# A long convolution, a LayerNorm and a two-row expert on one core: loads on one queue, a new order, two row writes

## The chip, the cores and the metric

The kernel runs on one core of one Trainium2 chip. The metric is the device time of one execution in microseconds. A core has five engines with their own instruction streams: PE (matmul, with PEld as its weight loads), DVE, ACT, POOL and SP, which here only issues DMAs. All inputs and the output are bfloat16 in HBM.

## The reference

S = 2048 tokens, D = 640 channels, F = 1728, four taps in the shift filter, two selected tokens.

```python
def _A_ref(q, k, v, shift_k, ssm_k, ssm_D):
    # k_shift: causal 4-tap filter along the tokens, one filter per channel
    kv = k_shift * v
    # y: causal convolution of kv with ssm_k along 2048 tokens, by FFT of length 2 S
    y = y + kv * ssm_D[None, None, :]
    return q * y

def _B_ref(x, w_r, w_gate, w_up, w_down):
    r = x @ w_r
    idx = jnp.argsort(-r, axis=-1)[:, :2]          # the two tokens of highest score
    g = _silu(x_sel @ w_gate); u = x_sel @ w_up
    y = (g * u) @ w_down * _sigmoid(r_sel)
    return x + scatter(y)                          # two rows change

h = A_q + _A_ref(_layernorm(A_q), A_k, A_v, A_shift_k, A_ssm_k, A_ssm_D)
h2 = h + _B_ref(_layernorm(h), B_w_r, B_w_gate, B_w_up, B_w_down)
```

`B_x` is not used.

## The kernel before

The 640 channels are worked in five chunks c of 128, and the tokens as 16 columns n2 of 128. The convolution is a transform of length 4096 in two steps each way, all as matmuls. For a chunk the groups of PE are: FT (transposes of the filter, 16 matmuls), S1f (first transform step of the filter, four groups of 16), KT (transposes of k), SC (the shift filter as matmuls with diagonal matrices, two groups), S1k (first step of k times v, four groups of 16), S2p (second step of both, eight groups of 16), I1 and I2 (the two inverse steps), T (transposes of h). Each group writes one of four PSUM regions; ACT or DVE then copies or multiplies the region into SBUF (`copyflex`, L334, recorded at L335). For chunk 0 the four taps use four diagonals. For chunks 1 to 4 two shifted copies of k are stacked in one tile (`Pst`); six SBUF to SBUF DMAs per chunk build them (`b_KT`), and SC needs all six. The filter spectrum is swapped between partition halves (`st_swap`, into KfB), by SP's DMA or DVE's copy for each half; DVE multiplies spectra (P1, P2). DVE and ACT make the first LayerNorm's sums of x (`ln0`), POOL normalises (L779). The last chunk's I2 goes in three parts of 8, 4 and 4 token columns (`LPARTS`), before and after.

The second LayerNorm's sums come from Gram matmuls (`b_G`, G0 to G4, small matmuls on transposed h, L822 and L827); G0 and G1 stand together after chunk 3's I1 groups. Then follow scores, the top two, the gather of the two rows by one-hot matmuls, the FFN (L1000, L1025), and `rows`, the two new rows. Meanwhile `outn` normalises all tokens, four bulk writes (`Dout`) store them, and `Dfix` writes the two rows over, when the bulk writes have landed.

Every step is declared once with the engines it may use (`decl`, `op`, `flex`, `dma`). The table `PLAN` then gives, step by step, the order, the engine and the PSUM region: an entry is 64 times the step's number plus 8 times the engine's number plus the region. `plan` derives the semaphore waits, `replay` emits each engine's stream. The order in an engine's stream is thus fixed: an instruction that waits holds all that stand behind it, SP's DMA issues too. In the diff `sp/act` lists the engines that a DMA may be issued from; the entry of `PLAN` says which it is.

Of the kernel before, what the change touches and what calls it, by code (L numbers as in the profile page):

```python
# [300 lines left out]
def build(nc, A_q, A_k, A_v, A_shift_k, A_ssm_k, A_ssm_D, B_x, B_w_r, B_w_gate, B_w_up, B_w_down, out):  # L301
# [8 lines left out]
    with es:  # L310
# [145 lines left out]
        def ld_filt(c):  # L456
            dma("sp/act", filt_C, A_ssm_k[CW * c:CW * c + CW, :], 1.35, writes=[buf("fC")], name="fC%d" % c)

        def ld_tok(c, nm, tile, src):
            w = min(2, NCH - c) * CW  # L460
            for i in range(2):
                a, b = 8 * i, 8 * i + 8
                dma("sp/act" if c == 0 else "sp", tile[:, a:b, 0:w], src[:, a:b, CW * c:CW * c + w], 1.75 if w > CW else 1.3,
                    writes=[buf(nm, j, i) for j in range(w // CW)], name="%s%d%d" % (nm, c, i), nd=1024)
# [7 lines left out]
        dma("sp/act", cons[:], I_d.ap(), 0.4, writes=[bI], name="cons")  # L472
# [4 lines left out]
        dma("sp/act/pool", tiny[:, 0:512], A_shift_k.rearrange("(c p) j -> c (p j)", c=NCH), 0.1, writes=[buf("ty", 0)] + bBp, name="wC", nd=5)  # L477
        dma("sp/act/pool", tiny[:, 512:640], A_ssm_D.rearrange("(c p) -> c p", c=NCH), 0.1, writes=[buf("ty", 1)], name="DC", nd=5)
        dma("sp/act/pool", tiny[:, 640:768], B_w_r.rearrange("(c p) -> c p", c=NCH), 0.1, writes=[buf("ty", 2)], name="wr", nd=5)
# [11 lines left out]
        dma("sp/act", F1[:].rearrange("p c k -> p (c k)"), F1_d.ap(), 0.4, writes=[bF1], name="F1")  # L491
        for h in range(2):
            dma("sp/act", F2c[:, 64 * h:64 * h + 64].rearrange("p k c m -> p (k c m)"), F2_d.ap()[:, 2048 * h:2048 * h + 2048], 1.4,
                writes=allq[0:4] if h == 0 else allq[3:7], name="F2c%d" % h)
# [645 lines left out]
```

## Time and profile before

| what | value |
|---|---|
| timed runs | 152.9, 154.67, 155.04 us (median 154.67) |
| profiled execution | 153.12 us, its span 151.3 us |
| busy PE, DVE, ACT, POOL | 118.6, 119.5, 111.2, 24.3 us |
| mean granted PE clock | 0.928 of full speed |
| moved by DMA | 29.54 MB, mean 195 GB/s |

The span is the time from the first to the last instruction of the program; the execution's own time has 1.8 us around it. Times in the profile count from the start of the span. Busy shares are averages over stages with different limits; the chain of waits says what ended last at each step.

### The profile page before, as it was taken

Reading aid. Unit: us, or ns where it says so; the run is one execution under the profiler, and the core shown is the slowest. Engines: PE = TensorE matmul, PEld = TensorE weight load, DVE = VectorE, ACT = ScalarE, POOL = GpSimd, SP = SyncE. Lnnn points to the kernel's source line nnn. Section 1 sums busy time; section 2 is a strip of 40 time slices with the busy share of each in tenths; the row PEclk is TensorE's granted clock in tenths of the full one; section 3 lists DMA queues with packets and bytes.
Section 4 is the critical chain, followed back from the end, with each engine's and each line's share of the span. In section 5 each row is a group of like instructions: output and inputs, shape, how many; then the busy total and the mean of one; then the engine's idle time right before and its main releaser. Section 6 shows DMA issues by size and latency. Waiting matters only on the chain.

```text
span 151.3 us, 6739 instructions
## 1 busy us (share of the span) xinstructions
PE 118.6 (78%) x3063; PEld 109.5 (72%) x3063; DVE 119.5 (79%) x186; ACT 111.2 (73%) x129; POOL 24.3 (16%) x29
## 2 busy tenths in 40 slices
PE   2504976895958879899999999998999199844991
PEld 2504975895947768799989899977999188733981
DVE  0379859997769997789888999889989465969812
ACT  0336999998559978899897998787999157229910
POOL 2003101005889994000000000000000000000000
PEclk9985799999999999999999999999999999995555
DMA  4999996999998838892659923378089950000970
GB/s 98 398 402 313 273 290 207 258 223 348 185 223 178 258 80 178 189 232 77 139 110 191 226 48 69 74 236 349 11 270 388 359 208 4 0 6 4 390 308 5
DMA packets 20900, 29.54 MB, mean 195 GB/s; under 512 B 5761, under 2 KB 16200, under 8 KB 20424
## 3 DMA queue, kind: packets, MB, share of 16 engines
q1 hardware_dynamic: 19566, 27.98, 64.1%
q10 hardware_dynamic: 1274, 1.13, 2.3%
q8 instruction: 24, 0.39, 1.1%
q14 instruction: 4, 0.03, 0.1%
q0 software_dynamic: 32, 0.00, 0.0%
HBM read 19.60 MB, written 2.62 MB: 147 GB/s over the span
## 4 chain that ended last, share of the span: by engine, by line
PE 56%; ACT 12%; DMA 11%; issue 9%; DVE 7%; SPq 3%; DVEq 0%; ACTq 0%
PE ps L600 10%; PE ps L644 7%; DMA x_sb<-in_A_q_dram 6%; PE ps L689 6%; PE ps L707 6%; PE ps L690 5%; PE ps L575 5%; ACT big L335 4%; DMA big<-big 4%; SPq L331 3%; PE ps L550 3%; PE ps L1000 3%; PE ps L581 2%; PE ps L728 2%; ACT A L335 2%
## 5 line engine op out<-in xcount | busy, mean ns | idle before, releaser
L335 ACT ACTIVATE big<-ps 128x1024 bf16<-128x1024 f32 (+2 forms) x40 | 42.6, 1112 | 7.5 <-PE ps L600 6.3
L335 ACT ACTIVATE A<-ps 128x1024 bf16<-128x1024 f32 x28 | 26.7, 1028 | 1.9 <-PE ps L644 1.9
L600 PE MATMUL ps<-F,big 128*64 128x128 bf16 x640 | 22.7, 221 | 4.3 <-issue 2.5
L644 PE MATMUL ps<-big,F 128*128 128x64 bf16 x640 | 21.5, 193 | 2.7 <-ACT big L335 1.3
L600 PEld LDWEIGHTS ps<-F,big 128*64 128x64 bf16 x640 | 18.7, 110 | 6.6 <-issue 2.9
L644 PEld LDWEIGHTS ps<-big,F 128*128 128x128 bf16 x640 | 19.8, 98 | 4.1 <-ACT big L335 2.0
L335 ACT ACTIVATE Bp<-ps 128x1024 bf16<-128x1024 f32 x17 | 16.9, 1035 | 7.9 <-PE ps L690 7.9
L779 POOL TENSOR_SCALAR q_sb<-x_sb,ln 128x640 bf16<-128x640 bf16 x16 | 19.5, 1218 | 11.5 <-DVE ln L776 10.0
L689 PE MATMUL ps<-G,A 128*128 128x128 bf16 x160 | 19.1, 219 | 0.2 <-ACT Bp L335 0.2
L690 PE MATMUL ps<-G,KfB 128*128 128x128 bf16 x160 | 19.0, 219 | 0.0
L717 DVE TENSOR_TENSOR atmp<-q_sb,ps 128x1024 bf16<-128x1024 bf16 (+1 forms) x11 | 12.3, 1122 | 5.5 <-PE ps L707 5.4
L689 PEld LDWEIGHTS ps<-G,A 128*128 128x128 bf16 x160 | 15.5, 98 | 0.9 <-ACT Bp L335 0.4
L690 PEld LDWEIGHTS ps<-G,KfB 128*128 128x128 bf16 x160 | 15.7, 98 | 0.0
L585 DVE TENSOR_TENSOR big<-ps,big 128x1024 bf16<-128x1024 f32 x10 | 12.2, 1224 | 4.2 <-PE ps L575 2.6
L335 DVE CAST A<-ps 128x1024 bf16<-128x1024 f32 x12 | 14.2, 1217 | 0.1
L665 DVE TENSOR_TENSOR A<-A 128x2048 bf16<-128x2048 bf16 x10 | 12.8, 1285 | 1.4 <-DMA KfB<-A 1.4
L707 PE MATMUL ps<-Bp,H 128*128 128x128 bf16 x160 | 10.7, 220 | 3.5 <-issue 3.0
L754 DVE BATCH_NORM_STATS2 st<-x_sb 128x6 f32<-128x320 bf16 x22 | 9.0, 479 | 4.0 <-DMA x_sb<-in_A_q_dram 4.0
L707 PEld LDWEIGHTS ps<-Bp,H 128*128 128x128 bf16 x160 | 9.0, 98 | 4.3 <-issue 3.2
L673 DVE TENSOR_TENSOR KfB<-A,KfB 128x2048 bf16<-128x2048 bf16 x10 | 12.1, 1217 | 0.0
L575 PE MATMUL ps<-diag,big 128*128 128x64 bf16 x256 | 8.6, 193 | 1.8 <-DMA big<-big 1.5
L335 ACT ACTIVATE q_sb<-ps 128x2048 bf16<-128x2048 bf16 (+2 forms) x5 | 7.4, 1472 | 3.1 <-PE ps L728 3.1
(119 smaller groups left out, 169.1 us busy)
## 6 DMA issues: line engine op xcount, KB each, us to landing
x_sb<-in_A_q_dram SPq DMA_DIRECT2D x4, 640.0 KB, 7.6
KfB<-A SPq DMA_DIRECT2D x5, 512.0 KB, 4.3
out_dram<-q_sb SPq DMA_DIRECT2D x4, 640.0 KB, 3.9
big<-big SPq DMA_DIRECT2D x8, 260.0 KB, 6.4
big<-in_A_v_dram SPq DMA_DIRECT2D x4, 512.0 KB, 8.1
big<-in_A_ssm_k_dram SPq DMA_DIRECT2D x4, 512.0 KB, 6.4
big<-big SPq DMA_DIRECT2D x8, 243.8 KB, 6.4
big<-in_A_k_dram SPq DMA_DIRECT2D x3, 512.0 KB, 8.7
```

The source lines that it names most:

```text
L335: return flex(lambda e: e.activation(o, i(), ACTF.Copy), lambda e: e.tensor_copy(o, i()), reads, writes, (t_act(n), t_d2(n) if bf else t_d ...
L575: return e.matmul(R32(bt)[:, o:o + 64], lhsT=lt, rhs=diagS[:, s, h, a, :], start=(a == 0), stop=(a == 1))
L585: op("dve", lambda e: e.tensor_tensor(kv[:, :, 8 * hb:8 * hb + 8, :], R32(bt).rearrange("p (n g l) -> p g n l", n=8, l=4), v_T[:, 8 * hb:8 ...
L600: return e.matmul(R32(bt)[64 * cc:64 * cc + 64, 128 * gl:128 * gl + 128], lhsT=lt, rhs=F1[:, cc, :], start=True, stop=True, tile_position= ...
L644: bt = op("pe", [lambda e, kl=kl: e.matmul(R32(bt)[:, 64 * kl:64 * kl + 64].rearrange("p (s g) -> p s g", s=2), lhsT=F2[:, 16 * r + kl, :] ...
L665: op("dve", lambda e: e.tensor_tensor(dst[:, :, blk], A[:, :, blk], dst[:, :, blk], ALU.mult), reads=[buf("A2", ksl(c), r) for r in rs], w ...
L673: return lambda e: e.tensor_tensor(K[:, g0:g1, blk], A[:, g0:g1, blk], K[:, g0:g1, blk], ALU.mult)
L689: ems.append(lambda e, g=g, gl=gl: e.matmul(R32(bt)[:, 128 * gl:128 * gl + 128], lhsT=dst[:, g, :], rhs=G[:, 0, :], start=True, stop=False))
L690: ems.append(lambda e, g=g, gl=gl: e.matmul(R32(bt)[:, 128 * gl:128 * gl + 128], lhsT=K[:, g, :], rhs=G[:, 1, :], start=False, stop=True))
L707: ems.append(lambda e, n2=n2, nl=nl, cp=cp: e.matmul(R32(bt)[:, 128 * nl:128 * nl + 128], lhsT=H[:, n2, cp, :], rhs=Bp[:, 16 * cp + n2, :] ...
L717: tr.decl({"dve": lambda e: e.tensor_tensor(at, qv, R32(bt)[:, 0:128 * nn].rearrange("p (n d) -> p n d", n=nn), ALU.mult)}, qb, ab, {"dve" ...
L779: lambda e, n2=n2: e.tensor_scalar(q_sb[:, n2, :], x_sb[:, n2, :], rd[:, n2:n2 + 1], nb[:, n2:n2 + 1], op0=ALU.mult, op1=ALU.add),
```

## The change

Four things are changed.

- The bulk loads (filter, first k and v, constants, the masks' source F2c, the weights) may now be issued by SP alone; the three tiny loads (`wC`, `DC`, `wr`) by ACT or POOL alone.
- `PLAN` is another table. It moves steps on all engines.
- The transposes of the two new rows (`YT`) are in two groups, of three and two, and their copy (`rows`) is in two: 384 columns on DVE, 256 on ACT.
- The row number of the second row is loaded on ACT, and ACT issues its write; SP keeps the first row.

```diff
 PLAN = [
-    32, 1248, 1744, 1424, 2960, 2832, 1120, 2512, 2896, 456, 1184, 1312, 536, 2384, 2704, 2576, 2448, 1472, 416, 577, 656, 720, 328, 5392, 5442, 2768,
...
+    1120, 1424, 392, 520, 2512, 2384, 2448, 2320, 1560, 1472, 1248, 3016, 472, 32, 577, 656, 10456, 1744, 720, 2896, 352, 5384, 1312, 3080, 3144, 800,
...
-            dma("sp/act", filt_C, A_ssm_k[CW * c:CW * c + CW, :], 1.35, writes=[buf("fC")], name="fC%d" % c)
+            dma("sp", filt_C, A_ssm_k[CW * c:CW * c + CW, :], 1.35, writes=[buf("fC")], name="fC%d" % c)
...
-                dma("sp/act" if c == 0 else "sp", tile[:, a:b, 0:w], src[:, a:b, CW * c:CW * c + w], 1.75 if w > CW else 1.3,
+                dma("sp", tile[:, a:b, 0:w], src[:, a:b, CW * c:CW * c + w], 1.75 if w > CW else 1.3,
...
-        dma("sp/act/pool", tiny[:, 0:512], A_shift_k.rearrange("(c p) j -> c (p j)", c=NCH), 0.1, writes=[buf("ty", 0)] + bBp, name="wC", nd=5)
+        dma("act/pool", tiny[:, 0:512], A_shift_k.rearrange("(c p) j -> c (p j)", c=NCH), 0.1, writes=[buf("ty", 0)] + bBp, name="wC", nd=5)
...
-        pt = op("pe", [lambda e, t=t: e.transpose(R16(pt)[0:2, 128 * t:128 * t + 128], yv[:, t, :], ident) for t in range(NCH)],
-                reads=[buf("yv", 0), buf("yv", 1), bI], region=True, dur=0.45, name="YT")
-        op("dve", lambda e: e.tensor_copy(rows, R16(pt)[0:2, 0:D]), writes=[buf("rows")] + bBp, uses=pt, dur=0.48, name="rows")
+        pt = op("pe", [lambda e, t=t: e.transpose(R16(pt)[0:2, 128 * t:128 * t + 128], yv[:, t, :], ident) for t in range(3)],
+                reads=[buf("yv", 0), buf("yv", 1), bI], region=True, dur=0.3, name="YT")
+        op("pe", [lambda e, t=t: e.transpose(R16(pt)[0:2, 640 + 128 * t:768 + 128 * t], yv[:, t, :], ident) for t in range(3, NCH)],
+           reads=[buf("yv", 0), buf("yv", 1), bI], writes=[buf("yt1")], uses=pt, dur=0.2, name="YT")
+        tr.decl({"dve": lambda e: e.tensor_copy(rows[:, 0:384], R16(pt)[0:2, 0:384])}, [], [buf("rows", 0)], {"dve": 0.32}, uses=pt, name="rows", after=bBp)
+        tr.decl({"act": lambda e: e.activation(rows[:, 384:D], R16(pt)[0:2, 1024:1280], ACTF.Copy)}, [buf("yt1")], [buf("rows", 1)], {"act": 0.38}, uses=pt, name="rows", after=bBp)
...
-            for cc in range(2):
-                t = tr.decl({"sp": lambda e, cc=cc: e.dma_start(out[0][bass.ds(vals[cc], 1), :], rows[cc:cc + 1, :])},
-                            [buf("rows")], [buf("fix", cc)], {"sp": 0.45}, dma=0.1, name="Dfix", after=[buf("outp", i) for i in range(4)])
+            for cc, g in enumerate(("sp", "act")):
+                def ldidx(e, cc=cc):
+                    vals[cc] = e.value_load(idxcol[cc:cc + 1, 0:1], min_val=0, max_val=S - 1)
+                t_ld = tr.decl({g: ldidx}, [buf("idxcol")], [], {g: 0.9}, name="LDI", silent=True)
+                t = tr.decl({g: lambda e, cc=cc: e.dma_start(out[0][bass.ds(vals[cc], 1), :], rows[cc:cc + 1, :])},
+                            [buf("rows", 0), buf("rows", 1)], [buf("fix", cc)], {g: 0.45}, dma=0.1, name="Dfix", after=[buf("outp", i) for i in range(4)])
```

The two helpers whose engine lists change alike (`F1`, `F2c`, `cons`, the weights `wg`, `wu`, `wd`) are left out.

What the table moves is seen in the engines' streams. SP at the start of the program; `in_A_q` is x, `in_A_ssm_k` the filter, `c_F2` the masks' source, `big<-big` a stack copy. Before:

```order
L331 DMA cons<-c_I 128x324
L331 DMA x_sb<-in_A_q_dram 128x2560 x4
L331 DMA Bp<-in_A_shift_k_dram 5x512
L331 DMA big<-in_A_k_dram 128x8x256
L331 DMA F1<-c_F1 128x256
L331 DMA q_sb<-c_F2 128x2048
L331 DMA big<-in_A_v_dram 128x8x256
L331 DMA q_sb<-c_F2 128x2048
L331 DMA big<-in_A_v_dram 128x8x256
L331 DMA big<-in_A_ssm_k_dram 128x2048
L331 DMA big<-in_A_k_dram 128x8x256 x2
L331 DMA big<-big 64x1950
```

After:

```order
L331 DMA x_sb<-in_A_q_dram 128x2560 x2
L331 DMA cons<-c_I 128x324
L331 DMA big<-in_A_ssm_k_dram 128x2048
L331 DMA x_sb<-in_A_q_dram 128x2560
L331 DMA F1<-c_F1 128x256
L331 DMA x_sb<-in_A_q_dram 128x2560
L331 DMA big<-in_A_k_dram 128x8x256
L331 DMA q_sb<-c_F2 128x2048
L331 DMA big<-in_A_k_dram 128x8x256
L331 DMA q_sb<-c_F2 128x2048
L331 DMA big<-in_A_v_dram 128x8x256 x2
```

The first filter chunk and half of the first k, which ACT issued before, are now in SP's row; behind the last row shown stand the second filter chunk, one k load (before: two) and the six stack copies.

PE at the start, behind its first transposes: L523 is FT, L545 and L550 KT, L600 S1, L581 SC of chunk 0. Before:

```order
L523 MATMUL ps<-cons,big 128x128 x16
L545 MATMUL ps<-cons,big 128x128 x16
L600 MATMUL ps<-F1,big 64x128 x48
L581 MATMUL ps<-diag,big 128x128 x32
L600 MATMUL ps<-F1,big 64x128 x16
L550 MATMUL ps<-cons,big 128x128 x16
L581 MATMUL ps<-diag,big 128x128 x32
L600 MATMUL ps<-F1,big 64x128 x64
```

After:

```order
L523 MATMUL ps<-cons,big 128x128 x16
L600 MATMUL ps<-F1,big 64x128 x48
L545 MATMUL ps<-cons,big 128x128 x8
L600 MATMUL ps<-F1,big 64x128 x16
L545 MATMUL ps<-cons,big 128x128 x8
L550 MATMUL ps<-cons,big 128x128 x16
L581 MATMUL ps<-diag,big 128x128 x64
L523 MATMUL ps<-cons,big 128x128 x16
```

The filter's S1 groups went ahead of the transposes of k, and chunk 0's two SC groups stand together.

SP near the end, the weights and the last swap. Before:

```order
L622 DMA KfB<-A2 64x4096
L331 DMA big<-in_B_w_gate_dram 128x3x1728
L331 DMA big<-in_B_w_up_dram 128x2x1728
L331 DMA big<-in_B_w_down_dram 128x4x640 x2
L331 DMA misc<-c_misc 128x320
L331 DMA big<-in_B_w_up_dram 128x3x1728
L331 DMA big<-in_B_w_down_dram 128x5x640
L331 DMA big<-in_B_w_gate_dram 128x2x1728
```

After:

```order
L622 DMA KfB<-A2 64x4096 x2
L331 DMA big<-in_B_w_gate_dram 128x2x1728
L331 DMA big<-in_B_w_down_dram 64x640
L331 DMA big<-in_B_w_down_dram 128x4x640
L331 DMA big<-in_B_w_up_dram 128x2x1728
L331 DMA big<-in_B_w_down_dram 128x4x640
L331 DMA big<-in_B_w_gate_dram 128x3x1728
L331 DMA big<-in_B_w_up_dram 128x3x1728
L331 DMA big<-in_B_w_down_dram 128x5x640
```

The first row of `w_down` waits for the last readers of the tile A1, the S2p groups of chunk 4, and holds the rows behind it; before, the two loads of `w_gate` and `w_up` stood ahead of that wait. Both halves of chunk 3's swap are DMAs now.

## Rows read from the trace of the kernel before

**Rows 1.** The page: busy us (share) xinstructions; a DMA queue's packets, MB, engines' share.

```profile
PE 118.6 (78%) x3063; PEld 109.5 (72%) x3063; DVE 119.5 (79%) x186; ACT 111.2 (73%) x129; POOL 24.3 (16%) x29
...
q8 instruction: 24, 0.39, 1.1%
```

**Rows 2.** Stages: length, busy us (xinstructions) PE, PEld, DVE, ACT, POOL; clock, DMA, GB/s.

```profile
25.00:37.00 12.00, 8.40 (x244) 7.78 (x244) 11.58 (x14) 11.94 (x12) 1.85 (x2) 1.00 1.04 285
...
45.00:62.00 17.00, 13.74 (x361) 12.46 (x360) 15.89 (x13) 15.01 (x16) 12.63 (x11) 1.00 0.74 176
...
62.00:98.00 36.00, 35.67 (x873) 33.47 (x871) 32.21 (x32) 32.05 (x34) 0.00 (x0) 1.00 0.61 135
```

**Rows 3.** Chain of waits, 0 to 37 us: start, length, what ended.

```profile
2.64 9.79 DMA x_sb<-in_A_q_dram
...
25.06 1.88 ACT big L335
...
30.45 6.29 DMA big<-big
```

**Rows 4.** Timeline of SP, 20 to 32 us: start, length, what it issued.

```profile
23.31 1.01 SPq L331 DMA_DIRECT2D big<-in_A_k_dram  x2
...
26.96 4.09 SPq L331 DMA_DIRECT2D big<-big  x6
```

**Rows 5.** Chain of waits, the whole span.

```profile
42.04 1.67 issue
...
49.26 0.36 issue
...
114.53 0.30 PE ps L822 x32
...
116.81 1.17 PE ps L707 x19
...
117.97 3.03 issue
```

**Rows 6.** DMA queues, 115.1 to 121 us: packets, MB, share of 16 engines.

```profile
q1 hardware_dynamic: 1023, 2.08, 98.3%
...
q8 instruction: 1, 0.02, 1.2%
```

**Rows 7.** DMA packets, 0 to 12 us.

```profile
DMA packets 1657, 3.62 MB, mean 301 GB/s; under 512 B 143, under 2 KB 1017, under 8 KB 1657
```

**Rows 8.** Groups by line and form: busy us, mean ns of one.

```profile
L335 ACT ACTIVATE big<-ps 128x2048 bf16<-128x2048 bf16 x4 | 7.5, 1884 | 1.0 <-PE ps L550 0.8 <-PE ps L581 0.2
...
L335 ACT ACTIVATE A<-ps 128x1024 bf16<-128x1024 f32 x28 | 26.7, 1028 | 1.9 <-PE ps L644 1.9
...
L335 DVE COPY big<-ps 128x2048 bf16<-128x2048 bf16 x5 | 6.1, 1223 | 1.8 <-PE ps L523 1.2 <-PE ps L550 0.6
...
L335 DVE CAST A<-ps 128x1024 bf16<-128x1024 f32 x12 | 14.2, 1217 | 0.1
...
L754 DVE BATCH_NORM_STATS2 st<-x_sb 128x6 f32<-128x320 bf16 x22 | 9.0, 479 | 4.0 <-DMA x_sb<-in_A_q_dram 4.0
```

**Rows 9.** The page's DMA issues: KB each, median us to landing.

```profile
KfB<-A SPq DMA_DIRECT2D x5, 512.0 KB, 4.3
```

**Rows 10.** Timeline of PE, 5 to 37 us.

```profile
14.08 1.93 PE L523 MATMUL ps<-cons,big 128*128 128x128 bf16 x16 [0.88 <-DVE big L521]
...
23.07 1.95 PE L581 MATMUL ps<-diag,big 128*128 128x128 bf16 x32
...
28.32 1.21 PE L523 MATMUL ps<-cons,big 128*128 128x128 bf16 x16
```

**Rows 11.** Timeline, from 139 us: the output writes and the row copy.

```profile
139.24 5.41 SPq L331 DMA_DIRECT2D out_dram<-q_sb  x4
...
148.68 0.48 DVE L1037 COPY Bp<-ps 2x640 bf16<-2x640 bf16 x1 [0.79 <-PE ps L1035]
...
149.34 0.72 SPq L1058 DMA_DIRECT2D out_dram<-Bp  x2
```

More of the change, by code (lines that the diff above doesn't have):

```diff
@@ L470, in ld_v @@
             ld_tok(c, "vT", v_T, v3)
-        dma("sp/act", cons[:], I_d.ap(), 0.4, writes=[bI], name="cons")
+        dma("sp", cons[:], I_d.ap(), 0.4, writes=[bI], name="cons")
         ld_k(0)
@@ L476, in build @@
         bBp = [buf("Bp", gb) for gb in range(4)]
-        dma("sp/act/pool", tiny[:, 0:512], A_shift_k.rearrange("(c p) j -> c (p j)", c=NCH), 0.1, writes=[buf("ty", 0)] + bBp, name="wC", nd=5)
-        dma("sp/act/pool", tiny[:, 512:640], A_ssm_D.rearrange("(c p) -> c p", c=NCH), 0.1, writes=[buf("ty", 1)], name="DC", nd=5)
-        dma("sp/act/pool", tiny[:, 640:768], B_w_r.rearrange("(c p) -> c p", c=NCH), 0.1, writes=[buf("ty", 2)], name="wr", nd=5)
+        dma("act/pool", tiny[:, 0:512], A_shift_k.rearrange("(c p) j -> c (p j)", c=NCH), 0.1, writes=[buf("ty", 0)] + bBp, name="wC", nd=5)
+        dma("act/pool", tiny[:, 512:640], A_ssm_D.rearrange("(c p) -> c p", c=NCH), 0.1, writes=[buf("ty", 1)], name="DC", nd=5)
+        dma("act/pool", tiny[:, 640:768], B_w_r.rearrange("(c p) -> c p", c=NCH), 0.1, writes=[buf("ty", 2)], name="wr", nd=5)
         ty4 = tiny[:, 0:512].rearrange("q (p j) -> q p j", j=4)
@@ L490, in build @@
         op("dve", lambda e: e.tensor_copy(D32[:], wDr[:, 8, :]), reads=[buf("DC")], writes=[buf("D32")], dur=0.17, name="D32")
-        dma("sp/act", F1[:].rearrange("p c k -> p (c k)"), F1_d.ap(), 0.4, writes=[bF1], name="F1")
+        dma("sp", F1[:].rearrange("p c k -> p (c k)"), F1_d.ap(), 0.4, writes=[bF1], name="F1")
         for h in range(2):
-            dma("sp/act", F2c[:, 64 * h:64 * h + 64].rearrange("p k c m -> p (k c m)"), F2_d.ap()[:, 2048 * h:2048 * h + 2048], 1.4,
+            dma("sp", F2c[:, 64 * h:64 * h + 64].rearrange("p k c m -> p (k c m)"), F2_d.ap()[:, 2048 * h:2048 * h + 2048], 1.4,
                 writes=allq[0:4] if h == 0 else allq[3:7], name="F2c%d" % h)
@@ L888, in build @@
                 WB[nm].append(bw)
-                dma("sp/act", wsb[:, a:b, :], src.rearrange("(t p) f -> p t f", p=128)[:, a:b, :], 1.1 * (b - a), after=wbufs(base + a * Ff, base + b * Ff), writes=[bw], name=nm, nd=128 * (b - a))
+                dma("sp", wsb[:, a:b, :], src.rearrange("(t p) f -> p t f", p=128)[:, a:b, :], 1.1 * (b - a), after=wbufs(base + a * Ff, base + b * Ff), writes=[bw], name=nm, nd=128 * (b - a))
         base = 2 * NCH * Ff
@@ L894, in build @@
             WB["wd"].append(bw)
-            dma("sp/act", wd_sb[:, a:b, :], B_w_down[128 * a:128 * b, :].rearrange("(t p) d -> p t d", p=128), 0.45 * (b - a), nd=128 * (b - a),
+            dma("sp", wd_sb[:, a:b, :], B_w_down[128 * a:128 * b, :].rearrange("(t p) d -> p t d", p=128), 0.45 * (b - a), nd=128 * (b - a),
                 after=wbufs(base + a * D, base + b * D), writes=[bw], name="wd")
@@ L898, in build @@
         WB["wd"].append(bw)
-        dma("sp/act", wd_sb[0:FL, NFT - 1, :], B_w_down[128 * (NFT - 1):Ff, :], 0.5, after=wbufs(base + (NFT - 1) * D, W_SZ), writes=[bw], name="wd")
+        dma("sp", wd_sb[0:FL, NFT - 1, :], B_w_down[128 * (NFT - 1):Ff, :], 0.5, after=wbufs(base + (NFT - 1) * D, W_SZ), writes=[bw], name="wd")
         for c in range(NCH - 1):
@@ L1049, in build @@
         if FIXSP:
-            vals = []
-            def ldidx(e):
-                for cc in range(2):
-                    vals.append(e.value_load(idxcol[cc:cc + 1, 0:1], min_val=0, max_val=S - 1))
-            t_ld = tr.decl({"sp": ldidx}, [buf("idxcol")], [], {"sp": 2.0}, name="LDI", silent=True)
-            t_fix = []
-            for cc in range(2):
-                t = tr.decl({"sp": lambda e, cc=cc: e.dma_start(out[0][bass.ds(vals[cc], 1), :], rows[cc:cc + 1, :])},
-                            [buf("rows")], [buf("fix", cc)], {"sp": 0.45}, dma=0.1, name="Dfix", after=[buf("outp", i) for i in range(4)])
+            vals = {}
+            t_fix = []
+            for cc, g in enumerate(("sp", "act")):
[4 more added lines that the diff above has]
+                            [buf("rows", 0), buf("rows", 1)], [buf("fix", cc)], {g: 0.45}, dma=0.1, name="Dfix", after=[buf("outp", i) for i in range(4)])
                 t.preds.add(t_ld.tid)
@@ L1063, in build @@
             t_fix = [tr.decl({"pool": lambda e: e.indirect_dma_start(out[0], bass.IndirectOffsetOnAxis(idxcol, 0), rows, None)},
-                             [buf("rows"), buf("idxcol")], [buf("outp", i) for i in range(4)], {"pool": 1.2}, dma=0.2, name="Dfix")]
+                             [buf("rows", 0), buf("rows", 1), buf("idxcol")], [buf("outp", i) for i in range(4)], {"pool": 1.2}, dma=0.2, name="Dfix")]
         if PLAN is None:
```

50 rows, old and new, of the table PLAN are left out of this document.

## The prediction

> **What bounds the kernel now.** I read the page first, then the table of stages, then the chain of waits stretch by stretch, and last the timelines of single engines. By the page [rows 1] PE is busy for 78% of the span, and DVE and ACT are close to it, so no engine alone is the bound. The stages [rows 2] tell where each one is: from 25 to 37 us ACT (11.94 of 12.00 us) and DVE (11.58) are full and PE waits for them; from 45 to 62 us DVE has 15.89 of 17 us and PE 13.74; from 62 to 98 us PE is full (35.67 of 36.00), so that nothing is to be had there.
>
> The chain of waits of the front [rows 3] shows what the first 37 us hang on: the last quarter of x, issued fourth and 9.79 us on the way; behind it, on ACT, four LayerNorm sums, half of the first k copy (the shift matmuls need it) and, at 25.06 us, the copy of the second k chunk; then six SBUF to SBUF copies that build the stacked tiles, the last of them 6.29 us on the way; and only then, at 36.94 us, PE's shift matmuls of chunk 1. The SP timeline [rows 4] shows why these copies land late: two more k loads, issued at 23.31 us, are just ahead of them.
>
> The pieces called "issue" in the same view [rows 5] are stretches in which PE waits for nothing that the profile shows. There are seven of PE's from 42 us on, the first 1.67 us, the last and longest 3.03 us at 117.97 us, in all 7.63 us. I take them for late instruction fetches. The page has 24 packets on an instruction queue, 0.39 MB [rows 1], hence 16 KB each; PE has 3,063 matmuls and as many weight loads, so a packet is some 255 PE instructions. Around the 3.03 us one such packet is in the list, while SP's queue q1 holds 98.3% of the DMA engines [rows 6].
>
> **Part 1, the front.** The new SP order brings the third quarter of x sooner, then k, and leaves one k load ahead of the stack copies instead of two. FT0 and its four S1 groups go ahead of the shift matmuls, which then stand back to back. Both halves of the first k copy move to DVE. Up to the second half of k, SP must move 4,753 KB, or 4.87 MB. The trace moved 3.62 MB in its first 12 us [rows 7], and 285 GB/s in the loaded stretch from 25 us [rows 2]: that half lands at 16.4 us. DVE gets there at about the same time: a first quarter of x at about 5 us (an estimate; it has the queue alone), 9.0 us for the 22 BN_STATS2 [rows 8], 1.22 for a filter copy and some 1.5 for small steps make 16.7; the two halves of the k copy then end near 18.2 us. Two shift blocks of 1.95 us [rows 10] end near 22.2 us, where the old ones, with two other groups between them, ended at 25.0. ACT has a mask expansion (1.9 us, from its copy of the same width) and a table load ahead of the second k copy, which I put at 22.6 to 24.5 us: 2.4 earlier than at present [rows 3]. The six issues take 4.09 us [rows 4]. The last copy lands 4.3 us after its issue if the queue is as empty as for the KfB copies [rows 9], 6.3 if it is as full as now [rows 3]. That is 32.3 to 34.4 us, where 36.75 is now. Chunk 1's shift matmuls start 2.3 to 4.4 us earlier, but two S1 groups that came before them (1.1 us) now come after. Net 1.2 to 3.3 us; I take **-3.0**, near the empty queue, since the one load left ahead is issued some 6 us before the copies. If PE's clock is low for the 64 shift matmuls (FT0 took 1.93 us, FT1 later 1.21, so 0.045 us for each matmul [rows 10]), 2.9 us go again. So the bounds of this part are 0 and -3.3.
>
> **Part 2, the copies from PSUM.** A 2048-wide transposed copy costs 1.88 us on ACT and 1.22 on DVE, a 1024-wide one 1.03 and 1.22 [rows 8]. ACT loses three of the first kind, one of 1.0 us and two S1 copies (2.06); it gains four S2 copies (4.11), an I1 copy (1.03) and the expansion (1.9): 1.7 us off. DVE gains two S1 copies and four transposed ones, one of them short, and loses four S2 copies, an I1 copy, an expansion and a swap: about 1.3 us off. From 25 to 62 us these two are the bound, beyond it PE is. I take **-1.0**, between 0 and -1.5. The swap of chunk 3 goes by SP in two halves, the second behind the first: some 8.6 us, twice 4.3 [rows 9]. It is hidden by the fifteen PE groups up to the last S1 copies, about 11 us; without that cover it would cost up to 2 us.
>
> **Part 3, late loads and fetches.** Old: 1,296 KB of wg and 864 KB of wu go early, 4.6 MB in one burst behind the last S2 group. New: 864 KB of wg goes early and 5.75 MB in the burst. At 285 GB/s [rows 2] it lasts some 20 us and ends by 127 us, ahead of the FFN at 141. The weights cost nothing. But the Gram sums of chunks 0 and 1 still stand together, with the same inverse groups behind them. The piece that was late begins at the same place of PE's order, and is now deeper in the burst. So the 3.03 us stay: 0. The piece before it may come late too: **+0.3**, between 0 and +1. The four stalls of the middle also keep their neighbours, H, the stack copies and v, and their pieces end within some tens of instructions of the old places. 0, between -3.6 and +3.
>
> **Part 4, the end.** Old [rows 11]: five transposes, a row copy of 0.48 us, then two row writes from SP, 0.72 us for both issues. New: three transposes and two; DVE copies 384 columns while ACT copies 256; SP and ACT write one row each. ACT's copy starts with the last transpose, as the old one did, and takes 0.4 to 0.5 us, so the first write is no earlier; the second is, by about 0.45. Loading the row number on ACT stands behind its last normalisation, 4 us ahead of its use. The row writes also wait for the bulk writes, whose last issue ends at 144.65 us [rows 11]; with the 4.3 us of the KfB copies [rows 9] that is 149.0, so no great gain can come out. **-0.5**, between 0 and -1.
>
> Moving bulk loads from ACT's queue to SP's is 0 by itself: the bytes are the same. The three tiny loads off SP let PE's first transposes start earlier, which is in part 1.
>
> **Sum.** -3.0 - 1.0 + 0.3 - 0.5 = -4.2 us on a profiled execution of 153.12 us: 148.9. The three timed runs are 152.9, 154.67 and 155.04; their mean with the profiled one is 153.93, so I add 0.8: **149.7 us**, 3.2% below the median of 154.67. About 2%, or 3.1 us, can be told from no change here: faster is below 151.6, slower above 157.8.
>
> **The rivals.**
> A, the forecast, 148 to 151.4 us: chance 0.54.
> B, the front's gain is given back in the middle. For it: an earlier front moves H, v and the stacks with it, and two more stalls of 1.5 us, like the 1.67 [rows 5], eat the 3.0; of part 2 half is left. Against: ACT and DVE are the bound there and get lighter. 153.9 - 0.5 - 0.5 = 152.9 us, chance 0.24.
> C, slower: a deeper SP queue makes every PE fetch as late as the worst of now. From the end of the first stall (43.71 us) to the next (49.26) PE had 5.55 us of work in a piece. Before the 3.03 us it had 19 inverse matmuls (1.17 us) and some 108 of the Gram sums (32 of the faster kind take 0.30 [rows 5], so I take 1.6), 2.8 us: that fetch took 5.8 us from one piece to the next. If the fifteen pieces from 37 to 118 us each took 6.6, they would stall by about 1 us, 15 in all, where it is 7.6 now. The change loses once the stalls grow by over 4.2 us; at +8 the time is 157.7. For: all bulk is on one queue, and the burst is bigger. Against: the bytes are the same, and most pieces come in time now. Chance 0.08.
> D, the order does what its name says, and half of the 7.63 us goes: 149.7 - 3.8 = 145.9 us, chance 0.14. Against: the largest stall keeps its place.
>
> Two rules of the Trainium skill bear on C and D. By "Runtime: NRT & Kernel Launch", section "Instruction fetch mechanics", an engine refills itself in blocks of 256 instructions while it runs, and crossing a block is mostly hidden; by that rule C and D would have no chance. The packet size of [rows 1] agrees; the 3.03 us of [rows 5] say that it is not hidden here. By "DMA: Bandwidth & Descriptors", section "Queues, rings and completion order", a DMA engine turns from queue to queue after each packet, so that the depth of SP's queue would not delay a fetch, and C would fall; a stall beside a q1 share of 98.3% [rows 6] speaks against relying on it.
>
> **How the numbers follow.** 149.7 is A's. The range 146.4 to 154.2 leaves out C, the upper edge of B and half of D, some 0.18. Faster is D and A up to its edge, 0.64; same is B and the rest of A, 0.28; slower is C, 0.08.
>
> **What would show it.** Right: chunk 1's shift matmuls start at 33 to 35 us, the first I1 group at 48 to 56 instead of 61.5, the last Gram group ends near 130.5 (134.3 now), and about 3 us of "issue" stand right behind the Gram sums of chunks 0 and 1. Wrong: the second k half lands after 18 us, PE's clock is still low beyond 19 us, PE's "issue" pieces sum to under 5 or over 10 us, or PE waits on the swap of chunk 3.

## The result and the profile after

The changed kernel took **149.83 us** (median of four runs, 149.11 to 153.23), beside 154.52 for the kernel before (four runs, 152.9 to 155.04): ratio 0.970, 95% interval 0.960 to 0.980. The profiled execution took 149.11 us, with a span of 147.3 us, 4.0 less than before. By that comparison it is faster, and 0.1 us from the forecast. Here and below a ratio compares, for each kernel, the runs near its fastest, while a median is over all runs. Two later comparisons, on chips 0 and 8 (the first pair's chip is not on record), did not give this gain again: their ratios are 1.002 and 1.015. So the number came out right for a reason that has to be taken apart.

The page of the changed kernel, to be held against [rows 1]: PE's busy time rose by 2.6 us though it does the same matmuls, and ACT's fell by 2.9.

```profile
PE 121.2 (82%) x3063; PEld 112.3 (76%) x3063; DVE 119.8 (81%) x185; ACT 108.3 (74%) x130; POOL 22.5 (15%) x29
...
q8 instruction: 24, 0.39, 1.1%
```

The table of stages, columns as in [rows 2], with a last stage of 8 us behind the Gram sums:

```profile
25.00:37.00 12.00, 10.33 (x310) 9.65 (x311) 10.67 (x13) 10.66 (x13) 6.15 (x7) 1.00 0.84 207
45.00:62.00 17.00, 14.59 (x372) 13.44 (x373) 16.11 (x14) 14.01 (x17) 5.38 (x5) 1.00 0.92 207
62.00:98.00 36.00, 35.78 (x908) 33.41 (x907) 32.82 (x32) 32.10 (x34) 0.00 (x0) 1.00 0.72 164
...
112.00:120.00 8.00, 4.79 (x57) 4.62 (x55) 4.69 (x5) 1.07 (x2) 0.00 (x0) 0.79 1.04 396
```

From 25 to 37 us ACT and DVE are no longer full, and PE does 1.9 us more work there. In the last row PE idles, with the DMA engines full and the granted clock at a mean of 0.79 (1.00 is the level of 2.4 GHz, 0.50 that of 1.2; a value between is the mean of a stretch that has both). The chain of waits says on what, as [rows 5] did; a piece of PE's called "issue" is called a stall from here on:

```profile
99.39 0.06 issue
...
112.70 3.21 issue
...
142.00 0.46 issue
```

The stalls at 42, 49, 54 and 61 us are gone, the one behind the Gram sums of chunks 0 and 1 stayed. The front, timeline of SP against [rows 4]: the six stack issues start 1.2 us earlier and take 4.44 us.

```profile
25.76 4.44 SPq L331 DMA_DIRECT2D big<-big  x6
```

They land 2.9 to 3.7 us after their issue, the last at 32.75 us. The end, against [rows 11]: two shorter row copies side by side, and two queues that write at the same time.

```profile
144.81 0.35 DVE L1039 COPY Bp<-ps 2x384 bf16<-2x384 bf16 x1 [0.57 <-PE ps L1035]
145.02 0.37 ACT L1040 ACTIVATE Bp<-ps 2x256 bf16<-2x256 bf16 x1 [4.65 <-PE ps L1037]
...
145.60 0.51 ACTq L1059 DMA_DIRECT2D out_dram<-Bp  x1
145.61 0.33 SPq L1059 DMA_DIRECT2D out_dram<-Bp  x1
```

I cut the span at four ends: of chunk 0's shift matmuls (line 581), of the last S2 group, of the last Gram group, and of the last transposes (line 1035 or 1037). The columns headed "again" and "third" are later executions of the same two kernels, on chip 0 and chip 8, profiled in the experiments.

| us | before | changed | before, again | changed, again | changed, third |
|---|---|---|---|---|---|
| front | 25.02 | 23.49 | 25.54 | 25.42 | 23.39 |
| to the last S2 group | **84.02** | 80.33 | 80.37 | 79.83 | 80.17 |
| to the last Gram group | 25.28 | 26.59 | 26.30 | 27.12 | 26.99 |
| to the last transposes | 14.31 | 14.57 | 14.52 | 14.22 | 14.60 |
| rest | 2.69 | 2.35 | 2.69 | 2.35 | 2.35 |
| span | 151.3 | 147.3 | 149.4 | 148.9 | 147.5 |

The first pair differs by -1.5, -3.7, +1.3, +0.3 and -0.3 us. The -3.7 comes from that execution of the kernel before. In its second trace the same program takes 80.37 us there, and the new order, unedited, 79.8 to 80.3. Set against the second trace, PE lost 4.3 us more to stalls in the first (4.61 beside 0.35: the four of the middle, 3.6 us, and two more of 0.28 and 0.70 us at 98.6 and 104.7) and 1.5 us more to the stack copies of chunk 1, but waited 2.2 us less for DVE and ACT (3.89 beside 6.09). The shift matmuls of chunk 1 in the first execution and in the second:

```profile
36.94 2.03 PE L575 MATMUL ps<-diag,big 128*128 128x64 bf16 x64 [1.53 <-DMA big<-big]
```
```profile
36.04 2.03 PE L575 MATMUL ps<-diag,big 128*128 128x64 bf16 x64
```

The new order is not free of this: a_warm, in experiment 8, has it unedited behind the front, and took 83.5 us there in its trace.

### The profile page after: what moved, and what is told of

Its sections match the earlier page's. It is cut to its first block, busy times and chain, and to the rows that moved or that the text cites. A ratio compares the mean times of both kernels' runs of the same rounds, so it can differ in the third digit from the quotient of the medians.

```text
span 147.3 us, 6739 instructions
## 1 busy us (share of the span) xinstructions
PE 121.2 (82%) x3063; PEld 112.3 (76%) x3063; DVE 119.8 (81%) x185; ACT 108.3 (74%) x130; POOL 22.5 (15%) x29
## 4 chain that ended last, share of the span: by engine, by line
PE 61%; DMA 14%; DVE 11%; ACT 6%; issue 4%; SPq 3%; DVEq 0%
PE ps L600 10%; PE ps L644 10%; PE ps L707 7%; PE ps L575 6%; PE ps L689 6%; DMA big<-in_A_ssm_k_dram 5%; DMA big<-big 5%; PE ps L690 5%; DVE big L335 3%; SPq L331 3%; DMA x_sb<-in_A_q_dram 3%; PE ps L523 3%; PE ps L728 3%; ACT Bp L335 3%; PE ps L1000 3%
## 5 line engine op out<-in xcount | busy, mean ns | idle before, releaser
L335 ACT ACTIVATE big<-ps 128x1024 bf16<-128x1024 f32 (+1 forms) x34 | 34.0, 1046 | 4.7 <-PE ps L600 4.4
L335 ACT ACTIVATE A<-ps 128x1024 bf16<-128x1024 f32 x32 | 30.4, 1031 | 3.1 <-PE ps L644 3.0
L335 ACT ACTIVATE Bp<-ps 128x1024 bf16<-128x1024 f32 x18 | 17.8, 1039 | 10.6 <-PE ps L690 10.5
L600 PE MATMUL ps<-F,big 128*64 128x128 bf16 x640 | 23.6, 230 | 2.1 <-DVE big L335 1.3
L600 PEld LDWEIGHTS ps<-F,big 128*64 128x64 bf16 x640 | 20.0, 116 | 4.2 <-DVE big L335 1.6
L689 PE MATMUL ps<-G,A 128*128 128x128 bf16 x160 | 20.2, 226 | 0.5 <-DVE A L665 0.5
L690 PE MATMUL ps<-G,KfB 128*128 128x128 bf16 x160 | 20.1, 225 | 0.0
L779 POOL TENSOR_SCALAR q_sb<-x_sb,ln 128x640 bf16<-128x640 bf16 x16 | 17.6, 1102 | 6.4 <-DVE ln L776 3.3
L335 DVE COPY big<-ps 128x2048 bf16<-128x2048 bf16 (+1 forms) x10 | 11.1, 1114 | 3.1 <-PE ps L545 1.3
L335 DVE CAST A<-ps 128x1024 bf16<-128x1024 f32 x8 | 9.6, 1218 | 0.8 <-PE ps L644 0.7
L335 ACT ACTIVATE q_sb<-ps 128x2048 bf16<-128x2048 bf16 (+2 forms) x5 | 6.1, 1220 | 4.4 <-PE ps L728 4.4
```

The lines of the kernel that those rows point to most:

```text
L335: return flex(lambda e: e.activation(o, i(), ACTF.Copy), lambda e: e.tensor_copy(o, i()), reads, writes, (t_act(n), t_d2(n) if bf else t_d ...
L600: return e.matmul(R32(bt)[64 * cc:64 * cc + 64, 128 * gl:128 * gl + 128], lhsT=lt, rhs=F1[:, cc, :], start=True, stop=True, tile_position= ...
L689: ems.append(lambda e, g=g, gl=gl: e.matmul(R32(bt)[:, 128 * gl:128 * gl + 128], lhsT=dst[:, g, :], rhs=G[:, 0, :], start=True, stop=False))
L690: ems.append(lambda e, g=g, gl=gl: e.matmul(R32(bt)[:, 128 * gl:128 * gl + 128], lhsT=K[:, g, :], rhs=G[:, 1, :], start=False, stop=True))
L779: lambda e, n2=n2: e.tensor_scalar(q_sb[:, n2, :], x_sb[:, n2, :], rd[:, n2:n2 + 1], nb[:, n2:n2 + 1], op0=ALU.mult, op1=ALU.add),
```

## The experiments

Theory 1: PE's stalls are instruction packets held behind bulk loads. In the traces a piece is 256 PE instructions: counted in order of time, matmuls and weight loads together, the four stalls of the middle stand behind 1217, 1473, 1729 and 1985 of them. I take it that the packet of the next piece is asked for when PE enters one; the profile does not show the request. The packet waits behind the bulk queue (the time from that entry to its start is its delay below), takes 0.9 to 1.5 us, and PE goes on 1.2 to 1.6 us after its end. A stall comes where that is longer than the piece's work. Theory 2: copies on ACT and DVE pace PE, and stalls only take the place of data waits.

**1. The last loads split in time (a_split).** wg's first part, wu's first part, wd's first and third part carry a wait on the Gram sums and stand behind them in SP's order. In the lines of SP, `wg3` is the part of w_gate from its block 3 of 128 rows on, and so with wu and wd; `|` stands before what waits for something.

```
+        HELD = {("wd", 9): [buf("gram", 0)], ("wg", 0): [buf("gram", 0)], ("wu", 0): ..., ("wd", 0): ...}
-  after=wbufs(base + a * Ff, base + b * Ff), writes=[bw], name=nm
+  after=wbufs(base + a * Ff, base + b * Ff) + HELD.get((nm, a), []), writes=[bw], name=nm
 SP: wg3 | wd13 wd5 wu3 | G1 done: wd9 wg0 | G3 done: wu0 wd0
```

> The changed kernel with its last loads split in time: 1.6 MB of the expert's weights goes out at 104 us as now, 1.9 MB only when the Gram group G1 has ended, 2.1 MB only when G3 has. Theory 1 (instruction packets held behind bulk loads): the stall of 3.21 us behind G0 and G1 falls under 0.5, the next packet's delay from 3.6 to under 1 us, and with the stall the low clock of 116 to 119.5 us goes too; PE then waits some 0.6 us for DVE in that place. Time 149.8 - 2.6 to 3.2 (stall) - 0 to 1.5 (clock) = 145.2 to 147.2, forecast 146. Rival (the stall is a price of the short Gram matmuls themselves, or DVE and ACT pace this stretch): the stall stays, or data waits of the same size take its place, 149 to 150.5. Second rival: the weights now land too late, FFN1 waits at 137 us, over 150.

Four runs, 146.62 to 153.29 us, median 149.17, profiled one 146.62; the kernel before took 150.73 there (150.1 to 152.22), and the changed kernel was not run there. The profiled run is near the forecast of 146, the median is not. From the start of G0 to the last Gram group it took 18.04 us where the changed kernel, in its first trace, took 21.17: 3.1 less. The stall went from 3.21 to 1.45 and not under 0.5, and the delay from 3.6 to 1.76 and not under 1: the first part was not yet in when PE entered the piece before, at 110.84 us. The DMA queues from there to PE's next instruction, packets, MB and share of 16 engines:

```profile
q1 hardware_dynamic: 402, 0.89, 63.4%
q8 instruction: 1, 0.02, 1.6%
```

In the changed kernel, over the same piece (109.9 to 116 us), the bulk queue never emptied:

```profile
q1 hardware_dynamic: 1043, 2.38, 102.7%
q8 instruction: 1, 0.02, 1.2%
```

**2. The same split in the kernel before (b_split).**

```
 SP: wg0 wu3 misc | wd5 | G1 done: wd9 wu0 | G3 done: wd0 wg3
```

> The kernel before with the same split alone (0.6 MB more before G0, then 1.9 MB behind G1 and 1.7 MB behind G3). Theory 1: the stall of 3.03 us at 117.97 falls under 0.5; as the clock did not fall there before, only the stall is won: 154.5 - 2.4 to 3.0 = 151.5 to 152.1. Rival (DVE and ACT pace this stretch, or the Gram matmuls themselves cost the stall): 154.0 to 155.

147.39 us, median of five (146.36 to 149.82), beside the same 150.73: ratio 0.970, interval 0.961 to 0.979. That is 3.3 us less, where 2.4 to 3.0 was said; the forecast time itself, 151.5 to 152.1, started from a kernel of 154.5. The stall is 0.38 us (packet delay 0.59), the Gram stretch 22.62 us. Theory 1 holds for this stall, since its rivals would have kept it. By these five and four runs the old kernel with the split is as fast as the new one with it, so the change itself shows no gain here.

**3. H back ahead of its neighbours (a_h_early).**

In the lines of SP, fC is a chunk's filter load, kT and vT are loads of k and v (chunk, half), sw is a swap, st a stack copy; G and H are the tables of the two inverse steps.

```
-SP: fC2 kT20 sw0 G H st2 ...
+SP: fC2 H kT20 sw0 G st2 ...
```

> The changed kernel with the load of the 1 MB table H put back where it was relative to its neighbours, right behind the filter of chunk 2 and ahead of the second k half of chunk 2, the first swap and G. Theory 1: the packet that PE asks for at 35.25 us waits over 3 us instead of 0.49, PE stalls 1 to 1.7 us near 40 us as the kernel before did at 42.04; the waits of 0.76 and 1.19 us for DVE at 42.9 and 45.7 us take up part of it, so the time is 150.0 to 151.5, forecast 150.4. Rival (the middle is paced by the copies, not by packets): no stall, or one wholly taken up by these waits, 149.4 to 150.0.

154.17 us, median of four (151.78 to 156.19), above the 150.0 to 151.5 of the forecast; profiled 154.23. The stall came, a piece earlier than I said: PE entered the piece before at 33.16 us, and the packet's delay was 3.49. Timeline of PE of this kernel (start, length, what; in brackets the idle time before):

```profile
36.80 0.69 PE L600 MATMUL ps<-F,big 128*64 128x128 bf16 x18
38.94 0.58 PE L600 MATMUL ps<-F,big 128*64 128x128 bf16 x14 [1.44 <-issue]
```

a_split, whose program is the changed kernel's up to 104 us, is its control on the same chip: it has no stall there, and from its last S2 group of chunk 0 to its second shift group of chunk 1 PE needs 1.6 us less. The waits for ACT and then DVE behind that are 0.78 and 1.18 us here, 0.77 and 1.18 in a_split: they took up nothing, they moved along. In this trace the stall's price is passed on whole, which speaks against theory 2's slack. It is not all of the time lost: against the changed kernel's first trace some 2 us were gone by the time H was issued, at 31.53 us. PE had waited 2.05 us for DVE, the granted clock was 0.50 from 27 to 30 us, and four S1 groups took 3.52 us, where the changed kernel's took 1.53 and 0.64.

**4. H late in the kernel before (b_h_late).** One half of chunk 2's v load moves with it.

```
-SP: fC2 H sw0 vT20 st2 st2 st2 st2 st2 st2 fC3 G
+SP: fC2 sw0 G H st2 vT20 st2 st2 st2 st2 st2 fC3
```

> The kernel before with H issued behind the first swap and G, and the v half of chunk 2 behind the first stack load, the order that the change has there, and nothing else. Theory 1: the stall of 1.67 us at 42.04 goes, perhaps those of 0.36 and 1.05 us behind it shrink; time 154.5 - 0.5 to 2.5 = 152.0 to 154.0, forecast 153.3. Rival (copies pace the middle): the stall goes and PE waits for DVE or ACT instead, 154.2 to 154.8.

157.21 us, median of four, ratio 1.038 (1.030 to 1.047): slower, which neither theory said. Timelines of SP and of PE:

```profile
40.00 0.44 SPq L331 DMA_DIRECT2D H<-c_H  x1
...
42.37 5.52 SPq L331 DMA_DIRECT2D big<-big  x5
```
```profile
55.35 1.87 PE L575 MATMUL ps<-diag,big 128*128 128x64 bf16 x32 [5.30 <-POOL q_sb L779]
```

POOL was long done; the last stack copy of chunk 2, behind H and v, landed at 54.89 us (52.01 in the kernel before, 49.53 in b_split), and PE idled 5.30 us for it. H and v moved together, so the run does not tell their shares. The order alone does not cost this either: the changed kernel has it too, its last stack copy of chunk 2 lands at 52.31 us, and PE, which does the first I1 group ahead of these shift matmuls, waits 0.16 us. What a place on SP's queue costs depends on what PE has to do meanwhile.

**5. Both kernels again (before_again, after_again).** No edit.

> The kernel before once more, unedited, profiled beside the others on this chip. Two kernels made from it ran on a chip where it took 150.7 us in place of 154.5, and their traces show no stall near 42, 49, 54 and 61 us though their loads up to 95 us were unedited in one of them: packets waited 1.7 to 2.2 us there instead of 3.2 to 3.5, and the stack copies of chunk 1 landed at 35.2 instead of 36.75. Theory 1a (the four stalls of the middle depend on how fast bulk loads drain in that execution): near 150.7 us none to one of the four stalls, near 154.5 us most of them. Rival (the stalls are fixed by the order of the program): four stalls whatever the time.

> The changed kernel once more, unedited, to compare the pair on one chip with a second trace. Theory 1a: the gain depends on how many stalls the kernel before has: where it takes 154 or more, ratio 0.965 to 0.975 as in the first comparison; where it takes 151 or less, the 3.6 us of the middle are not there to be won, and only the front (1 to 2 us), the copies and the tail (0.4) are left: 148.5 to 149.8, ratio 0.98 to 0.995. Rival (the gain is fixed): ratio 0.965 to 0.975 on either. In both the stall behind G0 and G1 stays at 3 to 3.5 us.

Kernel before: 152.85 us, median of 13 runs (149.23 to 162.65, and one of 274.72); profiled 151.21. Changed: 150.87, median of ten (149.49 to 153.43). Ratio 1.002 (0.993 to 1.010). The chain of waits of the kernel before, which had four stalls from 42 to 61 us:

```profile
53.36 0.19 issue
68.81 0.35 issue
...
114.83 2.83 issue
```

None of the four is left. What differs is how fast the loads drained, from 37 to 49 us, the same stretch of the same program, in the first execution and in this (one fence for each):

```profile
37.00:49.00 12.00, 9.69 (x270) 8.94 (x270) 8.97 (x8) 8.12 (x10) 10.96 (x12) 1.00 0.88 198
```
```profile
37.00:49.00 12.00, 10.38 (x291) 9.56 (x288) 10.95 (x10) 10.19 (x11) 10.96 (x12) 1.00 0.97 249
```

198 against 249 GB/s. H, issued at 32.07 and 32.75 us, landed at 42.71 and 40.94, and the late packets' delays were 3.2 to 3.5 us in the first, 1.3 to 2.0 in the second. A fixed gain of 3% falls. Theory 1a fits, on few traces: one of the old order that drained slowly, and this one and b_split (237 GB/s in this stretch) that did not; b_h_late, with H moved, had 211 GB/s and none of the four. The gain, none, is still less than theory 1a gave for either case.

**6. A smaller first part (a_split2).**

```
 SP: wg3 | wd13 wd5 | G1 done: wu3 wd9 wd0 | G2 done: wu0 wg0
```

> The split of the last loads with 0.9 MB less ahead of G0: 0.74 MB at 104 us, 2.36 MB behind G1, 2.65 MB behind G2 (the two weights that are read first lead). In a_split the packet for the piece behind G0 and G1 still waited 1.76 us behind the first part, and PE stalled 1.45 us. Theory 1: that packet now waits under 0.3 us, no stall, 0.7 to 1.2 us less than a_split, 3.7 to 4.5 us less than the changed kernel on the same chip: 145.0 to 145.8 where that takes 149.5. Rival (DVE and ACT pace the stretch from G0 on): no gain over a_split. If the weights now land too late, FFN1 waits at 135 us instead.

147.57 us, median of five (145.63 to 148.09), 3.3 under after_again where 3.7 to 4.5 was said. The stall is 0.28 us (delay 0.71, under 0.3 was said); another of 0.66 us stood behind G2 and G3.

**7. The copies back (a_copies, a_3copies).** All engines and regions by the new order; first 36 copies, then three, on the engine they had.

```
-DVE: FTc1 FTc2 KTc3
+ACT: FTc1 FTc2 KTc3
```

> The changed kernel with the 36 PSUM copies of chunks 0 to 4 that changed places between ACT and DVE put back on the engine they had before; order of every engine and of the loads as changed. The prediction gave the lighter ACT and DVE 1.0 us. Theory 1 (the middle is won by packets, and the copies sit beside PE work): 0 to +0.7 us over the changed kernel on this chip. Rival (theory 2, the copies pace PE between 36 and 100 us): +1.5 to +4 us, with waits of PE for ACT or DVE growing in the trace.

> The changed kernel with only the three wide transposed copies (FTc1, FTc2, KTc3) back on ACT, where each takes 1.88 us and not 1.22; all orders as changed. With 36 copies put back the time rose by 12 us, so PE does wait for copies. The prediction's part 2 gave all moves together 1.0 us (at most 1.5). By that: +0.3 to +1.0 over the control. Theory 2 (in the stretch up to 62 us ACT and DVE set PE's pace and each microsecond on ACT counts): +2 to +5, most of it before 60 us. Rival (slack takes it): under +0.3.

36 copies: 162.97 us, 12 over after_again; both theories missed it. Three: 155.55 (155.24 to 156.47), 3.9 over the median of the control of experiment 8, 151.65 (and 6.0 between the fastest runs, 155.24 and 149.28). Timelines of PE with three copies back, then of the control:

```profile
34.15 4.04 PE L644 MATMUL ps<-big,F 128*128 128x64 bf16 x80 [2.96 <-ACT big L335]
```
```profile
29.47 2.49 PE L644 MATMUL ps<-big,F 128*128 128x64 bf16 x80 [1.29 <-DVE big L335]
32.13 1.57 PE L644 MATMUL ps<-big,F 128*128 128x64 bf16 x48 [0.17 <-ACT A L335]
```

PE waits 2.96 us for an ACT copy and then works slower: 80 matmuls take 4.04 us where the control's 80 take 2.49. The granted clock of 34.1 to 38.2 us is 0.58. Theory 2 is right of this stretch: the copies do pace PE, and this wait lowered the clock as the stalls behind the Gram sums do. The 3.9 us are not the copies' alone: later in the middle the same trace has a wait of 1.32 us for stack copies and stalls of 0.48 and 1.31.

**8. A longer warm-up (a_warm), the control (after_third), and the longer warm-up with split loads (a_best).**

```
-R32(warm)[:, 0:128], lhsT=atmp[:, 0, 0, :], rhs=atmp[:, 0, 1, :]
+R32(warm)[:, 0:256], lhsT=atmp[:, 0, 0, :], rhs=atmp[:, 0, 1:3, :]
 a_best, SP: wg3 | wd13 wd5 | G1 done: wu3 wd9 | G2 done: wu0 wg0 wd0
```

> The changed kernel unedited, as the control for the three others on this chip. In the second comparison it took 150.87 us (149.49 to 153.43), in the first 149.83. Theory 1a (the gain over the kernel before is that kernel's own four stalls, where it has them, plus the front's 0 to 2 us by when PE's clock rises, plus 0.4 of the tail): 149.5 to 151, ratio 0.97 to 1.00 with the kernel before anywhere between 149.2 and 155. Rival (a fixed gain of 3%): ratio 0.965 to 0.975.

> The changed kernel with the 26 warm-up matmuls at the start widened from 128 to 256 columns (the same number of instructions), so that PE is at work from 1.1 to some 7 us and not to 4. In three traces of the changed front the S1 groups took 1.06 us each, as at half clock, and the groups took the full rate from 18.4 us in one, near 19 in another and 21.6 in a third; the last shift matmul of chunk 0 ended at 23.49, 23.97 and 25.42. Theory (the clock decides what the front is worth): the rate doubles before 17 us, that group ends at 22.0 to 23.0, and the time is 0.8 to 2 us under the unedited one's. Rival (the clock does not rise sooner, since PE still idles at 8.1 to 9.2 and 11.1 to 12.4 us): 23.5 to 25.4 as before, no difference within 0.5 us.

> The split loads and the wide warm-up together: 0.74 MB ahead of G0, 1.54 MB behind G1, 3.47 MB behind G2. In a_split2 a second small stall of 0.64 us stood behind G2 and G3 (packet 1.09 us late behind 2.36 MB); with 0.8 MB less ahead of it that one should go. Theory 1: no stall over 0.3 us behind either pair of Gram groups, last Gram group about 5 us earlier than in the changed kernel; 3.3 to 4.5 us less than it by the split, 0 to 2 more by the warm-up: 144 to 146.5. Rival: the later weights make FFN1 or FFN2 wait at 133 to 138 us, 147 or more.

Kernel before: 152.12 us, median of 23 (147.7 to 155.26). Control: 151.65, median of 12 (149.28 to 153.71), ratio 1.015 (1.001 to 1.028), where theory 1a had 0.97 to 1.00. a_warm: 151.41, median of 12 (149.16 to 153.99), no difference where 0.8 to 2 us less was said. **a_best: 146.59**, median of six (145.74 to 148.17), just over its forecast of 144 to 146.5; ratio to the kernel before 0.973 (0.963 to 0.984). By the medians it is 5.1 us under the changed kernel on that chip, by the fastest runs 3.5 (145.74 and 149.28), and its median is the lowest of all. Stages of the control, then of a_best:

```profile
112.00:120.00 8.00, 4.41 (x54) 4.22 (x51) 4.15 (x5) 0.72 (x2) 0.00 (x0) 0.79 1.04 397
```
```profile
112.00:120.00 8.00, 7.67 (x192) 7.17 (x188) 7.33 (x8) 4.62 (x5) 0.00 (x0) 1.00 0.57 193
```

PE does 7.67 us of work in these 8 instead of 4.41, and the clock stays. The weights were in time.

The warm-up did not decide when PE's rate doubles. The last S1 group of chunk 0 and the shift block in a_warm, then in a_best, which has the same warm-up:

```profile
16.20 0.64 PE L600 MATMUL ps<-F,big 128*64 128x128 bf16 x16
...
19.44 3.75 PE L581 MATMUL ps<-diag,big 128*128 128x128 bf16 x64
```
```profile
16.31 1.06 PE L600 MATMUL ps<-F,big 128*64 128x128 bf16 x16
...
21.10 4.10 PE L581 MATMUL ps<-diag,big 128*128 128x128 bf16 x64
```

a_warm's rate rose at about 16 us (granted clock 0.53 from 14 to 16 us, 1.00 from 16 to 18), a_best's only behind 20 (0.50 from 17 to 20). a_warm's front ended at 23.19, only 0.2 before the control: KT0 waits for an ACT copy until 18.05 us anyway. In the same trace the middle of the new order had what the first execution of the old one had, a late stack copy and a stall:

```profile
53.88 1.09 PE L575 MATMUL ps<-diag,big 128*128 128x64 bf16 x32 [1.63 <-DMA big<-big]
```
```profile
59.56 1.32 issue
```

Its loads moved 230 GB/s from 37 to 49 us; the three unedited executions of this order moved 251 to 252 and have neither.

## Why the prediction was right, and where it was not

- **The forecast of 149.7** met the first pair, whose spans differ by 4.0 us, against a sum of -4.2. Errors cancelled: against the sum's terms, the stages came out some 1.5 us worse in the front, 0.5 to 1 in the copies, 1 in the Gram stretch and 0.5 behind it, and 3.7 better in the middle by the stalls and waits of that execution. That they cancelled is luck. The four signs of being right all came true (33.75, 51.19 and 130.41 us, and a stall of 3.21), so they did not tell this sum from another; of the signs of being wrong, one did.
- **Part 3, the four stalls of the middle, "0": this step failed.** I took them for part of the program, kept by their neighbours. The traces showed them to be part of an execution: 3.6 us in the first trace of the kernel before, none of the four in its second, and one of 1.32 us in an execution of the new order. With them come late stack copies (waits of 1.53 and 1.63 us), which I had taken for the program's too. Part of this is paid back, since PE then waits less for DVE and ACT; what was left, 3.65 us between the two traces of the old order, is the first pair's -3.7 in the middle. My "issue" sum of 5 to 10 us was broken (3.21 + 0.46), as I had said would show it wrong.
- **Part 1, -3.0.** The second k half landed at 16.69 us (16.4 said), but the shift block ended at 23.49, not 22.2: the S1 groups ran at half rate, and KT0 waited 1.22 us for an ACT copy. The stack copies landed by 32.75 us, as forecast (32.3 to 34.4), and PE came to chunk 1's shift matmuls at 33.75 behind its own work. Behind chunk 1's shift groups and two S1 groups the first pair is 2.06 us apart. In after_again the full rate came only after 21 us and the front was worth 0.1; over all traces the new front ends at 23.19 to 25.42 us (ten), the old one at 25.02 to 25.54 (four). And the old stack copies were late in the first trace only: in before_again the last lands at 35.81 us and PE does not wait for it. The lower bound of 0, which I gave for a low clock, is what happened there; I should have made it a case with a chance.
- **Part 2, -1.0.** The middle takes 79.8 to 80.3 us new and 80.3 to 80.4 old where it has none of these stalls: 0 to -0.5. The copies pace PE, but old order with old engines and new with new come to the same.
- **Part 3, the burst, +0.3, and the 3.03 us that stay.** Right in place (112.70 us, right behind G1) and kind; 3.2 to 3.6 us in three traces. What I missed is PE's clock: after the stall the same groups took 1.4 to 1.5 us longer.
- **Part 4, -0.5.** -0.34 in each pair: right.
- **Rival D** had the right outcome for the stalls of the first pair (7.8 us of them before, 3.7 after) by the wrong reason, the order. **Rival B** is what the later pairs look like (-0.5 us of span from before_again to after_again), though nothing was given back: there was less to win. **Rival C** did not occur; a_h_early shows its mechanism, a fetch made late by a load ahead of it, at one place.

The Trainium skill's "Runtime: NRT & Kernel Launch", section "Instruction fetch mechanics", calls the crossing of a 256-instruction block mostly hidden. By the traces that is so for 20 of 23 crossings in the changed kernel (the others are the three pieces in its chain of waits above, 0.06, 3.21 and 0.46 us). It fails in all ten traces without held loads where a full bulk queue meets a piece that is mostly Gram matmuls (2.8 us of work), and in the first trace of the kernel before also at pieces of 4.6 to 5.5 us of work.

Still open: why the loads drained at 198 GB/s in that first execution, and how often it happens with either order. All four runs of the kernel before took 152.9 us or more in that comparison, where the changed kernel's median was 149.83; one was traced, so it is not shown that the others had these stalls, nor excluded that on that chip the old order drains slowly and the new one does not. On chip 8 the changed kernel's 12 runs lie closer together than the 23 of before, which suggests but does not show fewer stalls. Open too is what sets the time at which PE's rate doubles in the front.

## What to carry to other kernels

A stall that the profile calls "issue" may belong to an execution and not to the program: take a second trace of the unchanged kernel before pricing it, and compare spreads, not only medians. Where the stall comes back in every trace, look for a short stretch of many small instructions under a full load queue; holding the loads that are not yet needed until the stretch is over won 3.3 us in the old kernel and 3.3 to 5.1 in the new, by the medians. An order and an assignment of copies that were planned together are not to be priced one by one: three copies moved back cost 3.9 us, with a lower clock and late stack copies behind them.

## What the hardware showed that I had not expected

The clock's price of a stall is not in the stall. From the end of G1 to the end of T3 stand seven PE groups; less the stall between them they took:

| kernel | stall behind G0, G1 | rest up to T3 | granted clock from the stall to T3 |
|---|---|---|---|
| a_best, a_split2, b_split, a_split | 0.11, 0.28, 0.38, 1.45 | 6.93 to 6.94 each | 1.00 each |
| before (first) | 3.03 | 6.93 | 1.00 |
| before_again | 2.83 | 8.16 | 0.75 |
| changed, again, third | 3.21, 3.57, 3.60 | 8.30, 8.46, 8.31 | 0.76, 0.78, 0.79 |
| a_copies, b_h_late, a_3copies | 3.09, 3.30, 3.44 | 9.24, 8.17, 8.49 | 0.65, 0.76, 0.77 |
| a_h_early, a_warm | 3.53, 3.82 | 9.30, 9.25 | 0.64, 0.65 |

Up to 1.45 us of idling cost nothing more; around 3 us it cost 1.2 to 2.4 more in all but one. The granted clock behind it says so: 1.00 where nothing was lost, 0.64 to 0.79 where something was. At the front it does not always. It reads 1.00 from 15 to 17 us in the changed kernel (stages, columns as above), where an S1 group took 1.06 us that takes 0.64 later:

```profile
15.00:17.00 2.00, 2.00 (x28) 1.59 (x24) 1.93 (x7) 0.97 (x4) 0.00 (x0) 1.00 0.80 204
```

In a_split the same stretch, with an S1 group of the same 1.06 us, reads 0.50:

```profile
15.00:17.00 2.00, 2.00 (x26) 1.59 (x24) 1.93 (x7) 0.89 (x4) 0.00 (x0) 0.50 0.89 226
```

So in the first trace of the changed kernel it is the time of the groups, and not this reading, that shows the clock of the front.
